# First modulation of a spectral adaLN block folded into the Fourier table, grad_out transposes regrouped, x held on chip

## The chip, the cores and the metric

The kernel runs on one core of a Trainium2 chip. A core has five engines with a queue each: TensorE (PE, with its weight loads PEld), VectorE (DVE), ScalarE (ACT), GpSimd (POOL) and SyncE (SP), which issues most of the transfers. The metric is the device time of one execution in microseconds (us).

## The reference

The program returns the output of one block and its gradients for eight inputs, given `grad_out`. The block, cut to what matters:

```
mod = silu(c) @ w_mod                 # 6 vectors of 576: sa, ca, ga, sb, cb, gb
h = layernorm(x) * (1 + ca) + sa
x = x + ga * irfft2(rfft2(h) * (w_r + 1j*w_i))
h = layernorm(x) * (1 + cb) + sb
x = x + gb * (((h @ w_gate) * (h @ w_up)) @ w_down)
```

`x` and `grad_out` are 2048 x 576 in bfloat16, `w_gate` and `w_up` 576 x 4608, `w_down` 4608 x 576, `w_mod` 576 x 3456. The outputs are the block's result and the gradients of x, w_r, w_i, w_gate, w_up, w_down, c and w_mod.

## The kernel before, in words

The 2048 rows are dealt to 128 partitions and 16 tiles t, so that a tile is 128 rows by 576 columns. The Fourier transform over rows and columns is done as matrix products with tables.

**The head** (lines 288 to 461) is the part the change touches. The vector c is loaded (lines 291, 292), passed through the sigmoid, and spread over 128 columns per block of 128 values (`sc_rep`, line 308). `mod_load` (310) loads one sixth of w_mod as five blocks of 128 rows, `mod_make` (316) multiplies it, which gives a modulation vector repeated on all 128 partitions (`modh`), in two halves of 288 columns and five blocks each, thus ten products; it is also stored to memory (325) for later stages.

Then stage 1 runs as a software pipeline of three steps over the 16 tiles. `s1_norm` (359) takes the statistics of x (`norm_stats`, 175: six numbers per half row, a merge, a square root on ScalarE, a reciprocal and a product), normalises on ScalarE (372), multiplies by 1 + ca and adds sa on VectorE (374, 376), stores the normalised x (378), turns the tile with five transposes on PE (381) and copies it out on ScalarE (`hT`, 383). `s1_cols` (385) multiplies by the column table `RD`: ten products of 292 columns, five for the real and five for the imaginary part (390); ScalarE copies both to `zt` (391). `s1_rows` (400) multiplies by the row table `G1`, four products (404, 405), and ScalarE and VectorE copy one half each into `VA` (406). With tile 1, the gate vector gb is made too (394), stored, and read back as a column (`gbT`, 396 to 398).

**grad_out** is loaded in three pieces (349), turned tile by tile, six transposes each (421), and scaled by gb on VectorE into `goT` (422). A row has 576 = 4 x 128 + 64 columns; the fifth transpose gives the last 64 on partitions 0 to 63, and a sixth, of columns 448 to 575, gives them again on partitions 64 to 127, which line 423 scales. Later products for the upper blocks of w_down (from `TWICE` = 20 on) use the two copies side by side (444 to 447). In the earlier blocks the rows of w_down's transpose that meet the second copy are zero, from zeros that line 285 writes beside the loaded rows of `wdn`.

**After stage 1**, stage 2 turns each of 19 chunks of `VA` (477), transforms it (485), multiplies by the filter (492 to 497), turns it back (503) and transforms it back (511). Between the chunks groups of products goT x w_down (`u4_group`, 428; the product is line 451) fill PE; their result `ghh_st` goes to memory. Stage 3 (536 to 580) returns to rows (210 to 216), copies to `ut` (541, 542) and `yb` (552), and `s3_norm` (554) forms the second residual: it loads x again into `xc` (560), computes yb x ga + x (565, 566), takes statistics, normalises (570), and modulates into `h2p` (572 to 574). The long gated part follows, from line 583 to the end of its loop, and then the gradients' way back.

What sets the order: a scheduler places the instructions of each engine at build time from their data dependences and priorities. The function `in_order` (159) pins a list of one engine's instructions in the order given, and `issue_after` queues the instructions that its block traces on the same engine behind a given one; neither makes an engine wait at run time. `mod_make`'s store of the second vector is that instruction (`first`, 344) for most of SP's later loads. Transfers of the SP queue are issued in order, and one that must wait holds back those behind it.

## Time and profile before

| | |
|---|---|
| median of 3 runs | 1526.43 us (1525.81 to 1529.65) |
| profiled execution | 1524.87 us |
| its span, first to last instruction | 1523.1 us |
| mean granted TensorE clock | 0.996 |
| PE busy | 1490.3 us, 98% of the span |
| VectorE busy | 1060.6 us, 70% |
| ScalarE busy | 583.4 us, 38% |
| first column product of line 390 | 16.02 us |
| last, of tile 15 | 61.16 us |

How to read it: all times in a profile count from the first instruction of the profiled execution. A share of busy time is an average over the whole span; stages with different limits are read from the windows of the trace, which give each engine's busy time in a stretch. A line of the timeline gives start, duration, engine, source line, operation, output and inputs, and in square brackets how long the engine was idle before it and what ended the wait. A duration includes the time in which the next instruction has started already, so where a queue is full the distance from start to start is what an instruction costs.

### The profile page before, as it was taken

To read this page: it belongs to the slowest core of one execution; us is meant where nothing else is said; L and a number is where in the kernel's file an instruction comes from. 1 tells how busy PE (TensorE), PEld (TensorE's weight loads), DVE (VectorE), ACT (ScalarE), POOL (GpSimd) and SP (SyncE) were. 2 spreads that over 40 slices of the span, in tenths; PEclk is the share of its full clock that TensorE was granted. 3 is DMA by queue.
4 is the path that set the end of the run, shared out by engine and by line. 5 is a ranking of instruction groups with operands and counts; after the bars stand their busy time and mean duration, and the time that the engine had idled before them with its cause. 6 is when DMAs were issued, how large, how long until landed. Compare 5 with 4: busy or idle time off the path is not lost. (4 is left out here: it accounts for less than half of the span.)

```text
span 1523.1 us, 29031 instructions
## 1 busy us (share of the span) xinstructions
PE 1490.3 (98%) x11140; PEld 1012.6 (66%) x11144; DVE 1060.6 (70%) x2646; ACT 583.4 (38%) x1189; POOL 238.8 (16%) x363
## 2 busy tenths in 40 slices
PE   6899999999999999999999999999999999999998
PEld 4666543566666667666666676676666667888876
DVE  6866753666677767667677677676676768688884
ACT  6667742322222222222222222222222225686763
POOL 0001222101101102111111120120110113221022
PEclk9999999999999999999999999999999999999999
DMA  8968999688878768768778588688677779965587
GB/s 317 282 200 224 278 255 249 152 162 155 174 129 161 155 125 174 152 125 177 135 146 178 118 159 164 119 163 156 137 152 153 132 175 252 305 220 181 182 290 201
DMA packets 487181, 280.42 MB, mean 184 GB/s; under 512 B 408865, under 2 KB 457378, under 8 KB 486018
## 3 DMA queue, kind: packets, MB, share of 16 engines
q1 hardware_dynamic: 458882, 175.32, 55.6%
q0 software_dynamic: 28160, 103.25, 23.0%
q8 instruction: 87, 1.43, 0.4%
q14 instruction: 52, 0.43, 0.1%
HBM read 108.62 MB, written 82.31 MB: 125 GB/s over the span
## 5 line engine op out<-in xcount | busy, mean ns | idle before, releaser
L752 DVE TENSOR_TENSOR acc<-acc,u8p 128x288 f32<-128x288 f32 (+1 forms) x1088 | 483.3, 453 | 276.1 <-PE u8p L747 272.6
L747 PE MATMUL u8p<-wT,ggT 128*128 128x288 bf16 x1152 | 328.0, 286 | 1.7 <-DVE acc L752 1.6
L747 PE MATMUL u8p<-wT,guT 128*128 128x288 bf16 x1152 | 327.6, 286 | 0.0
L711 PE MATMUL gup<-h2T,wgu 128*128 128x512 bf16 x1152 | 297.8, 379 | 0.0
L646 ACT CAST so<-u57p 128x288 bf16<-128x288 f32 x216 | 86.3, 400 | 532.8 <-PE u57p L644 522.1
L644 PE MATMUL u57p<-h2p,gu_sf 128*128 128x288 bf16 x1152 | 186.4, 286 | 0.0
L644 PE MATMUL u57p<-h2p,gg_sf 128*128 128x288 bf16 x1152 | 185.9, 286 | 0.0
L711 PEld LDWEIGHTS <-wgu 128*128 128x128 bf16 x1152 | 109.6, 98 | 97.9 <-issue 17.1
L747 PEld LDWEIGHTS <-ggT 128*128 128x128 bf16 x1152 | 112.6, 98 | 66.5 <-issue 14.0
L451 PE MATMUL u4p<-goT,wdT 128*128 128x512 bf16 x656 | 151.1, 379 | 0.9 <-DVE goT L423 0.5
L747 PEld LDWEIGHTS <-guT 128*128 128x128 bf16 x1152 | 112.7, 98 | 57.6 <-issue 2.4
L1286 PE MATMUL u3p<-wd,hl 128*128 128x288 bf16 x936 | 141.3, 288 | 0.1
L713 ACT CAST gT<-gup 128x512 bf16<-128x512 f32 x144 | 84.5, 587 | 131.5 <-PE gup L711 129.6
L644 PEld LDWEIGHTS <-hh_sf 128*128 128x128 bf16 x1152 | 112.7, 98 | 28.4
L644 PEld LDWEIGHTS <-gu_sf 128*128 128x128 bf16 x1152 | 112.4, 98 | 28.5
L644 PEld LDWEIGHTS <-gg_sf 128*128 128x128 bf16 x1152 | 112.4, 98 | 28.2
L1286 PEld LDWEIGHTS <-hl 128*128 128x128 bf16 x1152 | 107.8, 98 | 25.7 <-DMA hl<-hhT_d 0.4
L713 ACT CAST uT<-gup 128x512 bf16<-128x512 f32 x144 | 84.5, 587 | 77.4 <-PE gup L711 77.4
L451 PEld LDWEIGHTS <-wdT 128*128 128x128 bf16 x656 | 61.3, 98 | 73.0 <-issue 7.6
L644 PE MATMUL u57p<-gonC,hh_sf 128*128 128x288 bf16 x576 | 99.7, 286 | 0.0
L724 POOL DMA_DIRECT2D hhT_d<-hhT x36 | 33.3, 925 | 375.5 <-DVE hhT L715 352.5
L173 DVE CAST ghh_st<-u4p 128x512 bf16<-128x512 f32 x56 | 38.7, 691 | 59.0 <-PE u4p L451 58.9
(373 smaller groups left out, 1867.6 us busy)
## 6 DMA issues: line engine op xcount, KB each, us to landing
ghhT_d<-ghh_st POOLq DMA_DIRECT2D x36, 512.0 KB, 4.3
ghh<-ghhT_d POOLq DMA_DIRECT2D x36, 512.0 KB, 7.3
hhT_d<-hhT POOLq DMA_DIRECT2D x36, 512.0 KB, 6.4
hl<-hhT_d SPq DMA_DIRECT2D x28, 576.0 KB, 6.0
out_dram<-woT SPq DMA_DIRECT2D x70, 128.0 KB, 2.0
wdn<-in_B_w_down_dram SPq DMA_DIRECT2D x18, 288.0 KB, 3.6
wd<-in_B_w_down_dram POOLq DMA_DIRECT2D x36, 144.0 KB, 4.7
out_dram<-so SPq DMA_DIRECT2D x36, 144.0 KB, 2.8
```

Of the source, the lines that this page charges most:

```text
L173: nc.vector.tensor_copy(dst, src)
L451: nc.tensor.matmul(pt[:], lhsT=wdTs[k][:, j, m, :], rhs=goT[:, 4 * sb4:4 * sb4 + 4, m, :], start=(m == 0 and n == 5), stop=(m == n - 1))
L644: mm = nc.tensor.matmul(pw[0][:, 0:288], lhsT=sf[:, t, :], rhs=rhs_n(t, h * 288, 288), start=(t == 0), stop=(t == NT - 1))
L646: followed(mm, nc.scalar.copy(so[:, h * 288:(h + 1) * 288], pw[0][:, 0:288]))
L711: nc.tensor.matmul(pts[k][:], lhsT=wgu[:, 4 * wi_ + m, jw * 128:(jw + 1) * 128], rhs=h2T[:, ts_, m, :], start=False, stop=(m == 3))
L713: nc.scalar.copy((gT, uT)[wi_][:, th_, :], pts[k][:])
L724: nc.gpsimd.dma_start(hhT_d[:, :, fb, :].rearrange("tp f x -> f tp x"), hhT[:].rearrange("f (tp ti) p -> f tp (ti p)", ti=2))
L747: nc.tensor.matmul(pu[:, 0:288], lhsT=l_, rhs=r_, start=(k == 0), stop=(k == len(mms) - 1))
L752: summed[t] = nc.vector.tensor_tensor(out=ghb(t)[:, hs_] if fbs[-1] == NFB - 1 else dst, in0=dst, in1=pu[:, 0:288], op=ADD).ins
L1286: mm = nc.tensor.matmul(p2[ti][:, 0:288], lhsT=hls[fb // 9][:, fb % 9, ti * 128:(ti + 1) * 128], rhs=w[:, fb - f0, h * 288:(h + 1) * 288], ...
```

## The change

- **The scale goes into the table, the shift into a row.** The normalised tile is no longer multiplied by 1 + ca and shifted by sa. Instead the column table is scaled, row by row, by 1 + ca (`RDs`), which is possible because the table's rows are the tile's columns. To have 1 + ca and sa along partitions, new products with one moving column each are made (`mod_cols`, 25 per vector). The tile buffers `n1r` have ones in columns 576 and 608, which become rows 64 and 96 of the fifth block, and the table gets there the product of sa with `RD`, in two bfloat16 parts. The repeated vector 1 + ca is still made and stored; the repeated sa is not.
- **grad_out is turned five times instead of six.** Tiles whose number divided by four is odd take columns 448 to 575 in the fifth transpose, the others columns 512 to 639, and `gbT` holds a scale column for each case, with zeros where the other half lies, so one scaling per tile remains. `gbT` now comes from one-column products and no longer from memory. The last 64 rows of w_down's blocks are therefore loaded twice in all blocks, not only from the twentieth on.
- **x stays on chip.** All of x is loaded into `h2p`, which stage 3 reads in place of `xc`.
- Beside these: 56 products of the unit matrix with itself at the start, whose result is not used; `G1` loaded in two parts; the copies of line 406 moved to VectorE for half of the tiles; the order of PE in the prologue and of some of VectorE's instructions pinned; the sigmoid ahead of the first square root.

```diff
+        n1r = [hw2.tile([128, 4, DP], BF, name="n1r%d" % k, bufs=1) for k in range(2)]
+        for n_ in n1r:
+            nc.gpsimd.memset(n_[:, :, D:DP], 0.0)
+            nc.gpsimd.memset(n_[:, :, D:DP:32], 1.0)
...
+        warm = fps.tile([128, 512], FP32, name="warm", tag="fp")
+        with tc.high_priority(60):
+            for _ in range(56):
+                nc.tensor.matmul(warm[:, 0:128], lhsT=ident[:], rhs=ident[:], start=True, stop=True)
...
+        def mod_cols(wm):
+            ps = fps.tile([128, 512], FP32, name="modc", tag="fp")
+            for d in range(5):
+                w = min(128, D - 128 * d)
+                for m in range(5):
+                    nc.tensor.matmul(ps[0:w, d:d + 1], lhsT=wm[:, m, 128 * d:128 * d + w], rhs=sc_bf[:, m:m + 1], start=(m == 0), stop=(m == 4))
+            return ps, ((slice(0, 128), slice(0, 4)), (slice(0, 64), slice(4, 5)))
+
+        def x_load(t0, t1):
+            nc.sync.dma_start(h2p[:, t0:t1, 0:D], x_v[:, t0:t1, :])
...
+        def scaled_table():
+            ps, parts = mod_cols(wms[MCA])
+            for r, k in parts:
+                one = nc.vector.tensor_scalar(out=opca_c[r, k], in0=ps[r, k], scalar1=1.0, scalar2=None, op0=ADD)
+            for m in range(5):
+                r = slice(0, min(128, D - 128 * m))
+                nc.vector.tensor_scalar(out=RDs[r, m].rearrange("p c f -> p (c f)"), in0=T["RD"][r, m].rearrange("p c f -> p (c f)"), scalar1=opca_c[r, m:m + 1], scalar2=None, op0=MUL)
+            return one.ins
+
+        def shift_rows():
+            ps, parts = mod_cols(wms[MSA])
+            for r, k in parts:
+                nc.vector.tensor_copy(msl[r, k, 64:128:32], ps[r, k].unsqueeze(2).to_broadcast([r.stop, k.stop - k.start, 2]))
...
+            for cc in range(2):
+                zp = fps.tile([128, 512], FP32, name="zms", tag="fp")
+                for m in range(5):
+                    nc.tensor.matmul(zp[:, :FP], lhsT=msl[:, m, :], rhs=T["RD"][:, m, cc, :], start=(m == 0), stop=(m == 4))
+                nc.scalar.copy(RDs[64:65, 4, cc, :], zp[64:65, :FP])
+                nc.vector.tensor_copy(hi[96:97, cc, :], zp[96:97, :FP])
+                nc.vector.tensor_tensor(out=RDs[96:97, 4, cc, :], in0=zp[96:97, :FP], in1=hi[96:97, cc, :], op=SUB)
...
-            nm = hw2.tile([128, D], BF, name="nm")
-            nc.vector.tensor_tensor(out=nm[:], in0=n1[:, tt, :], in1=modh[MCA][:], op=MUL)
-            hh = hpp[:, t % 3, :]
-            nc.vector.tensor_tensor(out=hh[:, 0:D], in0=nm[:], in1=modh[MSA][:], op=ADD)
...
-                    mm = nc.tensor.matmul(zp[:, :FP], lhsT=hTs[t][:, m, :], rhs=T["RD"][:, m, cc, :], start=(m == 0), stop=(m == 4))
+                    mm = nc.tensor.matmul(zp[:, :FP], lhsT=hTs[t][:, m, :], rhs=RDs[:, m, cc, :], start=(m == 0), stop=(m == 4))
...
-                evac(Vv[:, :, t, cc, :], vp[:, :FP].rearrange("k (g f) -> k g f", f=4), eng=("a" if cc == 0 else "v"))
+                evac(Vv[:, :, t, cc, :], vp[:, :FP].rearrange("k (g f) -> k g f", f=4), eng=("a" if cc == 0 and t % 2 else "v"))
+
+        s1_norm(0)
+        mod_make(MCA, wms[MCA])
+        mark1 = traced()
+        shift_rows()
+        dve0 += on_dve(mark1)[0:2]
+        s1_cols(0)
+        in_order(pe_since(mark))
+        mark = traced()
+        pipeline(NT, [lambda t: s1_norm(t) if t else None, lambda t: s1_cols(t) if t else None, s1_rows])
+        in_order(dve0 + on_dve(mark)[0:9])
...
-            pt = u4ps.tile([128, 6, 128], BF, name="u4p")
-            for m in range(6):
-                nc.tensor.transpose(pt[:, m, :], gon(t, m * 128 if m < 5 else 448, 128), ident[:])
-            nc.vector.tensor_tensor(out=goT[:, t, :, :], in0=pt[:, 0:5, :], in1=gbT[:].unsqueeze(2).to_broadcast([128, 5, 128]), op=MUL)
-            nc.vector.tensor_tensor(out=goT[64:128, t, 4, :], in0=pt[64:128, 5, :], in1=gbT[64:128, 4:5].to_broadcast([64, 128]), op=MUL)
+            odd = t // 4 % 2
+            pt = u4ps.tile([128, 5, 128], BF, name="u4p")
+            for m in range(5):
+                nc.tensor.transpose(pt[:, m, :], gon(t, m * 128 if m < 4 or not odd else D - 128, 128), ident[:])
+            nc.vector.tensor_tensor(out=goT[:, t, :, :], in0=pt[:], in1=gbT[:, odd, :].unsqueeze(2).to_broadcast([128, 5, 128]), op=MUL)
...
-                    if fb >= TWICE:
-                        nc.sync.dma_start(wdn[:, :, D:DP], rows[:, :, 512:D])
+                    nc.sync.dma_start(wdn[:, :, D:DP], rows[:, :, 512:D])
...
-            xc = hw2.tile([128, 2, D], BF, name="xc")
-            nc.sync.dma_start(xc[:], x_v[:, s0:s0 + 2, :])
...
-                nc.vector.tensor_tensor(out=x1[:, i, :], in0=x1[:, i, :], in1=xc[:, i, :], op=ADD)
+                nc.vector.tensor_tensor(out=x1[:, i, :], in0=x1[:, i, :], in1=h2p[:, s0 + i, 0:D], op=ADD)
```

More of the change, by code (lines that the diff above doesn't have):

```diff
@@ L295, in build @@
         sig = hp1.tile([128, 5], FP32, name="sig")
-        nc.scalar.activation(out=sig[:], in_=c_f[:], func=ACT.Sigmoid)
-        nc.vector.tensor_tensor(out=sc_col[:], in0=c_f[:], in1=sig[:], op=MUL)
+        gated = nc.scalar.activation(out=sig[:], in_=c_f[:], func=ACT.Sigmoid).ins
+        sc_bf = hp1.tile([128, 5], BF, name="sc_bf")
+        nc.vector.tensor_tensor(out=sc_bf[:], in0=c_f[:], in1=sig[:], op=MUL)
         tmp5 = hp1.tile([128, 5], FP32, name="tmp5")
@@ L302, in build @@
         nc.vector.tensor_tensor(out=dsl_col[:], in0=tmp5[:], in1=sig[:], op=MUL)
-        sc_bf = hp1.tile([128, 5], BF, name="sc_bf")
-        nc.vector.tensor_copy(sc_bf[:], sc_col[:])
         nc.vector.tensor_copy(sc_col[:], sc_bf[:])
@@ new lines, in build, with s1_stats, on_dve @@
+        n1s = {}
+        def s1_stats(t):
+            n = 1 if t == 0 else 4 - t % 4
+            nmr = norm_stats(h2p[:, t:t + n, 0:D], hw2, n, "ln1", rstd1g[:, t:t + n], 4)
+            for k in range(n):
+                n1s["nmr", t + k] = nmr[:, k:k + 1]
+        def on_dve(mark):
+            return [i for i in nc.cur_bb.bb.instructions[mark:] if i.engine == mybir.EngineType.DVE]
+        mark = traced()
+        s1_stats(0)
+        nmr0 = on_dve(mark)[-1]
+        in_order([gated, rooted[0]])
@@ L394, in s1_cols @@
                     mod_make(MGB, wms[MGB], "a")
-                with nc.allow_non_contiguous_dma(reason="tiny column load"):
-                    nc.sync.dma_start(gbT[:, 0:4], modb_d[0, MGB, 0:512].rearrange("(m q) -> q m", q=128))
-                    for r in (0, 64):
-                        nc.sync.dma_start(gbT[r:r + 64, 4:5], modb_d[0, MGB, 512:576].rearrange("(m q) -> q m", q=64))
+                ps, parts = mod_cols(wms[MGB])
+                for r, k in parts:
+                    for odd in range(2):
+                        if k.start < 4 or not odd:
+                            nc.vector.tensor_copy(gbT[r, odd, k], ps[r, k])
+                ps = fps.tile([128, 512], FP32, name="modc", tag="fp")
+                for m in range(5):
+                    nc.tensor.matmul(ps[:, 0:1], lhsT=wms[MGB][:, m, D - 128:D], rhs=sc_bf[:, m:m + 1], start=(m == 0), stop=(m == 4))
+                nc.vector.tensor_copy(gbT[64:128, 1, 4:5], ps[64:128, 0:1])
         def s1_rows(t):
```

80 lines of the change are left out of this document (41 added, 39 removed).

## The prediction

> **What bounds the kernel now.** I cut the span into stages first, at the start of the first column product (16.00), of the third (24.95), of the last (61.16), and at the first turn of a filtered chunk (76.04, line 503). The columns are the stretch, its length, and the busy us of PE, PEld, DVE, ACT and POOL, then the granted clock, the DMA share and GB/s.
>
> ```profile
> 0.00:16.00 16.00, 5.15 (x25) 2.96 (x25) 9.10 (x42) 8.33 (x13) 1.57 (x12) 0.97 0.85 298
> 16.00:24.95 8.95, 8.49 (x53) 5.75 (x54) 5.71 (x19) 5.08 (x12) 0.71 (x1) 0.68 1.03 385
> 24.95:61.16 36.21, 32.99 (x300) 24.23 (x301) 31.68 (x84) 30.98 (x67) 3.37 (x5) 1.00 0.94 292
> 61.16:76.04 14.88, 12.54 (x105) 7.53 (x103) 11.90 (x26) 5.96 (x12) 0.53 (x1) 1.00 0.80 271
> 76.04:160.00 83.96, 83.96 (x655) 51.83 (x654) 54.94 (x158) 58.26 (x118) 10.76 (x20) 1.00 0.76 218
> 160.00:200.00 40.00, 37.59 (x248) 23.11 (x247) 29.44 (x96) 30.39 (x63) 10.29 (x19) 1.00 1.08 276
> ```
>
> PE is full from 76.04 to 160 and nearly full afterwards, so whatever time PE saves before 76.04 lasts to the end. The order of PE's matmuls in the built kernels is the same in both from that turn on. There are two places to gain: the head, and the idle 2.4 us of 160 to 200. For the second, PE's waits there, and the wait for the tile `xc`:
>
> ```profile
> PE yp L216 <- ACT ut L171: 1.8, 2, 1.3
> PE yp L216 <- DVE ut L173: 0.6, 1, 0.6
> ```
> ```profile
>   DMA xc<-in_A_x_dram: 5.0, 4
> ```
>
> VectorE waits four times, 5.0 us together, for x read a second time (line 560); `ut` and the norms queued behind line 566 come late, and PE with them.
>
> Inside the middle stage one tile costs 2.53 us at best, and that is a loop between ScalarE and PE, not PE's work. In the timeline:
>
> ```profile
> 30.98 1.42 PE L390 MATMUL zp<-T_RD,hT 128*128 128x292 bf16 x10
> ...
> 32.43 0.40 ACT L171 CAST zt<-zp 128x292 bf16<-128x292 f32 x1 [0.22 <-PE zp L390]
> ...
> 32.77 0.69 ACT L171 COPY hT<-trp 128x640 bf16<-128x640 bf16 x1
> ...
> 33.51 1.42 PE L390 MATMUL zp<-T_RD,hT 128*128 128x292 bf16 x10
> ```
>
> Products at 30.98, second `zt` 1.45 later, `hT` 0.34 after it, next products 0.74 after that: 2.53. A normalisation (line 372, 0.77 from start to start) ahead of the first `zt` fits into ScalarE's idle time; one between the two `zt` lengthens the loop.
>
> **The head, walked anew.** Durations are rows of this execution; the order of each engine is that of the built kernel.
>
> *A, to the second tile's norm.* The removed steps are the 20 products of line 320 for the first two vectors (10 stay), the shift of line 376 and the scale of line 374 (32 VectorE operations, 14.6 us). Their place is taken by 56 warm-up products while PE idles for loads (the first products of before started at 6.85; 56 at the cold pitch of 0.11 end near 7.5), then 25 one-column products for each vector, five table scalings, ten products of the shift row with the table and six small row operations. A one-column product I take at 0.06, the warm start-to-start of line 381's 128-column transposes, between nothing less than that weight load and the cold 0.11. Column products of the first vector run 7.4 to 8.9; transposes, 10 products (1.22) and the second vector's columns end at 12.1. A scaling of 584 elements has no row: from 0.22 (line 308) to 0.82 (line 422); I take 0.25, as both operands lie in SBUF as in line 308. The table lands near 11.0 (12.06 in before, now with 432 KB less ahead), scalings end at 12.2, the ten products at 13.9. VectorE then has a statistic of tile 4 queued ahead of the row operations, and that waits for x of tiles 4 to 7: 3,706 KB into a queue that moved 1,536 KB from 12.06 to 15.74, thus 14.4. From there copy (0.46), statistic (0.39), subtraction (0.46), twice, end at 17.25, so the first column product is complete at 17.4, against 18.6. But the statistics of tiles 1 to 3 now follow: seven operations to 19.1, square root 0.30, reciprocal, statistic, product to 20.2; normalisation 0.87; transposes of tile 1 start at **21.0**. In before they started at 18.4.
>
> *B, 21.0 to the third column product.* PE has no gap: 5 transposes 0.30, four row products 0.49, 8 transposes of grad_out 0.49 (the load is due at 20.7: 6,154 KB, where before had 6,442 KB at 21.9), column product 1.22, ten products of the gate vector 1.22, 30 one-column products 1.80, transposes 0.30, row products 0.49, 7 transposes 0.43: 6.74 at full clock. The clock is the doubt:
>
> ```profile
> 8.08:11.49 3.41, 2.90 (x13) 1.67 (x12) 3.09 (x11) 0.17 (x1) 0.00 (x0) 1.00 1.10 434
> 11.49:14.90 3.41, 1.02 (x10) 0.48 (x7) 1.46 (x7) 3.23 (x6) 0.00 (x0) 1.00 0.96 402
> 14.90:18.32 3.42, 2.30 (x10) 1.46 (x11) 2.43 (x6) 2.24 (x4) 0.71 (x1) 0.50 1.03 349
> 18.32:21.73 3.41, 3.41 (x19) 2.12 (x18) 1.55 (x5) 1.73 (x4) 0.00 (x0) 0.50 1.05 359
> ```
>
> A stretch of 3.41 us with PE busy 1.02 was followed by half clock; 2.30 did not end it, 3.41 did, and 2.90 had released it earlier. In A, PE works about 1.2 us between 14.0 and 21.0, so half clock is due when B starts, and it lasts until a stretch that PE fills, beginning somewhere in the 3.4 us after about 20.2, has passed: 1.4 to 3.1 lost, mean 2.2. The third product starts at 21.0 + 6.7 + 2.2 = **29.9** (before: 24.95). The Trainium skill, "TensorE: Matmul & The Clock Gate", section "What's actually happening", says that the clock is halved after at least one idle window of about 3.4 us in a free-running grid. Read as a wholly idle window it would hardly ever strike here and B would lose nothing; the trace's window with 1.02 busy speaks against that reading.
>
> *C, third to last column product.* By ScalarE's order: five loops with two normalisations or one between the `zt`s (3.0, 2.92, 3.0, 3.0, 2.70), the other eight at 2.53: 34.9. VectorE's 16 statistics (0.39) and its other rows from 29.3 put the fourth grad_out product at 41.6, and PE's ten transposes queued there wait about 1.0 (nothing to 2.0). So 35.9 (before 36.2), and the last product starts at 65.8. The loop of ScalarE stays; that is where the 14.6 us of VectorE go: beside it.
>
> *D, last product to the turn at 76.04.* Before, 33 of 96 grad_out transposes were still to come and PE waited for lines 422 and 423; the 30 products of line 451 followed them. After, all 80 are done, line 423 (16 at 0.29) is gone and two of the 30 products too: last row products 2.27 in, 15 products 3.34, 4 transposes 0.25, 4 products 0.89, 0.50, 6 products 1.34, 0.50: 9.1, against 14.9. The turn comes at **74.9**: the head gains **1.1**.
>
> *Queues.* SP now issues x of tiles 4 to 7 and the rest of the row table ahead of the second half of the prologue, since they stand behind an instruction of VectorE and no longer behind the stores of line 325. The gate vector's load waits for its buffer until PE's ten products at 10.4, the grad_out loads behind it; with 4,858 KB issued by then the transfers do not run dry. The gate vector's store (needs ScalarE, near 28) holds x of tiles 12 to 15 to a landing near 33; VectorE wants it near 36. The three column loads of `gbT` and SP's 6.1 us wait for them go; its values now come from the 30 one-column products in B. POOL's six added memsets are short (0.14 to 0.30 in its rows) and over before 4. The eight evacuations of line 406 moved from ScalarE to VectorE (0.46 each) are in C's sums.
>
> **x kept.** The eight loads of `xc` go and with them the 5.0 us of VectorE's waits; PE's 2.41 idle go if no other wait is next. From 184 on, with `xc` early, a tile takes 3.93 without a gap, ScalarE's and VectorE's work fitting in. I take **2.4** (bounds 0 and 2.4). The ten added loads of 64 columns (0.47 of the SP queue, 3.5 to landing in line 438's rows) precede transposes whose result is ready near 53 and wanted near 60: nothing, unless they were 7 us later.
>
> **Sum.** 1.1 + 2.4 = 3.5. The profiled execution took 1524.87 (span 1523.1), so 1521.4 of that kind; the median of the runs shown, 1526.43, is 1.56 higher: **1522.9**. About 0.3%, 4.6 us, is what a measurement can tell from no change.
>
> **Rivals.**
> 1. *The clock stays full.* For it: the warm-up products, and column products filling PE until 12.1. Against: the window of 1.02. B loses nothing, the head gains 3.3, but VectorE's wait in C takes 0 to 1 more; in all 5.7: 1520.7.
> 2. *Slower: one-column products do not count as work for the clock.* They use one column of the moving operand, and no row shows one. Place: half clock from about 11, so the second vector and the row products take 1.85 longer ahead of 17.25, and B stays cold throughout, 6.7 lost instead of 2.2. That is 6.4 worse, 1529.3; it decides once more than 3.5 us beyond my 2.2 are lost. Against: 128-column weight loads run all along, and the longer products between them are counted.
> 3. *x kept does nothing:* the norms then wait for the next thing, the ScalarE order around line 570. Head alone: 1525.3. Against: all three PE waits follow a wait for `xc`.
>
> **Chances.** Forecast 0.50 (0.14 of it over 4.6 faster, 0.01 slower), rival 1 0.25 (0.22 faster), rival 2 0.15 (half of it slower by 4.6, 0.07), rival 3 0.10 (0.01 slower). Faster 0.36, same 0.55, slower 0.09. For the range: forecast ±2 from the clock's phase, the wait in C and the scalings (0.25 to 0.82 costs up to 1.9 behind the landing at 14.4), extended to rival 1 with a short wait below and over rival 3 above: 1519.3 to 1527.0; the far part of rival 2 stays out.
>
> **What would show it.** The first column product complete near 17.4 and tile 1's transposes near 21; half clock over the third product's approach; third product 29.9, last 65.8, first turn 74.9; no wait for `xc` and no idle PE between 160 and 200. A third product before 28, or one after 32, or PE waits of another name in the norms would prove the sum wrong.

## The result and the profile after

The changed kernel takes 1521.61 us (median of 8 executions, 1519.33 to 1524.64), the kernel before beside it 1530.11 (8 executions, 1524.49 to 1535.08): ratio 0.9946 (95% interval 0.9925 to 0.9968). It is **faster, by 0.54%**, a small gain; a ratio of 1 lies outside the interval. The time foretold, 1522.9, is 1.3 above the median and the range holds it; but the gain in medians is 8.5 us where the sum said 3.5. The two profiled executions differ by only 1.4 us (1523.45, span 1521.7, against 1524.87, span 1523.1). So the sum was right neither about the medians nor about that pair, and the question is why in both.

First the stages of the changed kernel. They are cut at 16.00 as before, and then where the prediction's steps end: tile 1's transposes start at 22.60 (end of A), the third column product at 30.11 (B), the last at 65.11 (C), the first turn at 74.10 (D). The columns are those of the first table of the prediction: stretch, length, busy us of PE, PEld, DVE, ACT, POOL, granted clock, DMA share, GB/s.

```profile
0.00:16.00 16.00, 11.96 (x135) 9.80 (x135) 6.16 (x35) 6.34 (x10) 2.96 (x17) 0.89 0.86 306
16.00:22.60 6.60, 1.22 (x6) 0.51 (x7) 6.41 (x22) 2.02 (x5) 0.00 (x0) 0.73 1.05 415
22.60:30.10 7.50, 7.50 (x83) 6.10 (x83) 3.19 (x13) 6.01 (x12) 0.91 (x1) 0.78 0.73 257
30.10:65.10 35.00, 33.84 (x316) 25.29 (x315) 25.99 (x64) 27.44 (x58) 2.82 (x4) 1.00 0.97 284
65.10:74.10 9.00, 8.96 (x63) 5.05 (x62) 3.69 (x10) 4.66 (x10) 1.77 (x2) 1.00 0.74 253
74.10:158.10 84.00, 84.00 (x654) 51.83 (x655) 56.87 (x165) 58.95 (x120) 11.90 (x22) 1.00 0.83 230
158.10:198.10 40.00, 40.00 (x262) 24.63 (x261) 32.10 (x102) 32.03 (x65) 10.83 (x20) 1.00 1.08 272
```

The last row answers to 160 to 200 of before: PE busy 40.00 of 40.00 instead of 37.59, and in PE's waits none is left for `yp`. The first turn is 1.94 earlier (74.10 against 76.04). The last product of stage 3 comes 4.9 earlier (start of the last `yp` product 194.73 against 199.60), and the gated products (lines 770 and 775) start 5.2 earlier, 267.60 against 272.78. That lead is still whole 990 us later, at the first column sum with `n2c` (line 979): 1256.78 against 1261.98. But the span is only 1.4 shorter. The rest of the lead is lost **after** 1256, in two places (3.1 and 1.6; after them 0.9 comes back, as the part behind 1486 takes 35.5 instead of 36.4). The first is in PE's waits (engine, line and operation, what it waited for; us, times, longest), at the top of the list:

```profile
PE csC L979 <- DMA yc<-y_d: 2.9, 1, 2.9
PE trp L434 <- ACT n1r L429: 2.8, 1, 2.8
PE spp L991 <- ACT dmb L1003: 2.7, 1, 2.7
PE zp L443 <- DVE RDs L387: 2.7, 2, 2.1
PE zms L384 <- DVE msl L379: 2.3, 1, 2.3
```

The first line has no counterpart in before: PE waits 2.9 for one load of `yc`, and the column sums take 69.92 from first to last instead of 66.86. The second place is the clock. The third line, a wait that before has too (2.4), leaves PE idle near 1470. In stretches on the clock's own grid, after and then the changed kernel with whole rows (an experiment below):

```profile
1469.70:1473.10 3.40, 1.36 (x10) 0.78 (x7) 3.26 (x9) 0.00 (x0) 1.37 (x2) 1.00 1.06 404
1473.10:1476.50 3.40, 2.72 (x9) 1.71 (x10) 3.26 (x10) 3.14 (x6) 0.00 (x0) 0.50 0.75 238
1476.50:1479.90 3.40, 3.40 (x16) 2.11 (x14) 2.51 (x7) 3.32 (x7) 0.57 (x1) 0.50 0.73 229
```
```profile
1465.90:1469.30 3.40, 1.81 (x13) 1.14 (x11) 3.26 (x9) 0.00 (x0) 1.56 (x2) 1.00 1.08 406
1469.30:1472.70 3.40, 2.53 (x18) 1.96 (x19) 3.26 (x9) 2.95 (x6) 0.00 (x0) 1.00 0.78 257
1472.70:1476.10 3.40, 3.40 (x30) 2.71 (x28) 2.54 (x8) 3.32 (x7) 0.37 (x1) 1.00 0.74 243
```

About the same idle time lies inside one stretch in the first (1.36 busy, then half clock for two stretches) and across two in the second (1.81 and 2.53 busy, clock full). From the last of those column sums to the first `spp` product of `dsa` (line 991) it takes 156.2 in the second kernel, 157.9 in before (one stretch at half clock) and 159.5 in after (two). All fourteen profiles lie between 156.2 and 159.7. In twelve of them that wait is 2.3 to 2.7, and the time goes by the number of stretches at half clock alone: 156.2 or 156.3 with none (four profiles), 157.7 to 158.1 with one (seven), 159.5 with two (after). The two kernels without the warm-up products wait 3.5 and 3.8 and take 159.4 and 159.7 with one. So the second place is where the grid stands against the idle time in that execution, and not something that the change did. The Trainium skill, "TensorE: Matmul & The Clock Gate", section "What's actually happening", says that the window is about 3.4 us long and free-running; these rows agree. It gives an idle window as the cause of half clock; here 1.36 busy us in the window did not prevent it.

### The profile page after: what moved, and what is told of

It reads as the page before. It is cut to its first block, busy times and chain, and to the rows that moved or that the text cites. A ratio compares the mean times of both kernels' runs of the same rounds, so it can differ in the third digit from the quotient of the medians.

```text
span 1521.7 us, 29239 instructions
## 1 busy us (share of the span) xinstructions
PE 1495.4 (98%) x11260; PEld 1020.0 (67%) x11264; DVE 1048.5 (69%) x2620; ACT 580.3 (38%) x1182; POOL 241.0 (16%) x368
```

## The experiments

**The theories after this result.** X: `xc` costs more than the 2.4 of one profile, because the time of its loads differs from execution to execution. The rival is that the head gives the rest. In the first two recorded expectations X is called rival A; their own theory T, that the profiled pair tells the whole gain and that its late loss is chance, is the first thing to be tested. For the late loss, P: the five memsets that the change added on POOL shift its queue. R: the change makes POOL's queue hand out more rows, which moves a pause of that queue. Medians below are of as many executions as are given; before ran beside each group (medians 1525.88 to 1528.98, single executions 1521.37 to 1537.74).

### x kept alone, and x not kept

**Only x kept** (before, with this one part of the change):

```diff
-            xt = hw2.tile([128, 4, D], BF, name="xt", bufs=3)
+            xt = h2p[:, 4 * c4:4 * c4 + 4, 0:D]
...
-            nc.sync.dma_start(xc[:], x_v[:, s0:s0 + 2, :])
...
+                nc.vector.tensor_tensor(out=x1[:, i, :], in0=x1[:, i, :], in1=h2p[:, s0 + i, 0:D], op=ADD)
```

> The kernel before with one part of the change: all of x is loaded into h2p and stage 3 reads it there; xc and its eight loads are gone. Theory T (the lead of the profiled pair at the start of the gated part, 5.2 us, is the lasting gain: 1.9 from the head and about 3.0 from stage 3; what the pair lost again after 1257 us, 2.9 in a wait for yc and 1.7 in one more stretch of half clock, is chance of one execution): first turn of a filtered chunk at 76.0 as before, no PE wait for ut, last product of stage 3 (yp) at 196.6 in place of 199.6, and 3.0 us less than before in the medians. Rival A (the eight loads cost much more in most executions than in the profiled one, which is why the medians differ by 8.5): 6 to 8 us less than before, and a narrower spread of its times. Rival B (x kept does nothing, the norms wait for the next thing): within 1 us of before, yp at 199.

Measured: 1519.28 (1518.49 to 1519.96, 12), ratio 0.9952 (0.9933 to 0.9971); before beside it 1526.52. That is 7.2 us, three times the term of the sum. The spread fell from 16 us (before, 35 executions) to 1.5. Theory T had the events right (last `yp` product at 196.5, foretold 196.6, no wait for `ut`), but its 3.0 for the medians is refuted.

**x reloaded** (after, with that part undone):

```diff
+            xc = hw2.tile([128, 2, D], BF, name="xc")
+            nc.sync.dma_start(xc[:], x_v[:, s0:s0 + 2, :])
...
-                nc.vector.tensor_tensor(out=x1[:, i, :], in0=x1[:, i, :], in1=h2p[:, s0 + i, 0:D], op=ADD)
+                nc.vector.tensor_tensor(out=x1[:, i, :], in0=x1[:, i, :], in1=xc[:, i, :], op=ADD)
```

> The changed kernel, but stage 3 loads x again into xc as before. Theory T: first turn at 74.1 as in the changed kernel, VectorE waits for xc some 5 us and PE for ut some 2 to 3 us, last yp at 197.7; 1.9 us less than before in the medians, about 3 more than the changed kernel. Rival A (the loads of xc are what mattered): 0 to 2 us less than before, 6 to 8 more than the changed kernel. Rival B: the same as the changed kernel, 5 to 8 less than before.

Measured: 1526.00 (1522.98 to 1530.29, 12), ratio 0.9990 (0.9971 to 1.0010): without x kept nothing measurable is left of the change. (This kernel has the head's gain and the late loss too, so it says nothing of either alone.) VectorE's timeline of this kernel (start, us, line, operation, in brackets the idle time before it and what ended it), and PE's waits:

```profile
142.78 0.46 DVE L632 TENSOR_TENSOR x<-x,xc 128x576 bf16<-128x576 bf16 x1 [4.81 <-DMA xc<-in_A_x_dram]
...
183.01 0.46 DVE L632 TENSOR_TENSOR x<-x,xc 128x576 bf16<-128x576 bf16 x1 [1.49 <-DMA xc<-in_A_x_dram]
...
194.82 0.46 DVE L632 TENSOR_TENSOR x<-x,xc 128x576 bf16<-128x576 bf16 x1 [4.16 <-DMA xc<-in_A_x_dram]
```
```profile
PE yp L218 <- ACT ut L171: 3.3, 3, 1.3
PE yp L218 <- DVE ut L173: 3.3, 2, 2.3
```

The same eight loads in the same stage: VectorE waits 12.9 us in four places where the profile of before had 5.0 in four, PE 6.6 where before had 2.4, and a load lands after 6.5 (median; longest 10.3) instead of 4.9 (6.4). The DMA share of that stage is 1.1, so a reload takes what the other transfers leave it. From the first to the last `yp` product the stage takes 63.0 in before, 67.5 here, and 60.0 or 60.1 in every kernel with x kept. X holds: one part of the change, in the old head, gives 7.2 of the 8.5, so the rival falls. That the time of the loads differs so much is read from two profiles and from the spread of the run times; which other transfers hold them up stays open.

### The head

**grad_out turned six times again** (after, with the fifth and sixth transpose, the second scaling, and w_down's second load only from the twentieth block on):

```diff
+        nc.gpsimd.memset(wdn2[:, :, :, D:DP], 0.0)
...
-            pt = u4ps.tile([128, 5, 128], BF, name="u4p")
-            for m in range(5):
-                nc.tensor.transpose(pt[:, m, :], gon(t, m * 128 if m < 4 or not odd else D - 128, 128), ident[:])
+            pt = u4ps.tile([128, 6, 128], BF, name="u4p")
+            for m in range(6):
+                nc.tensor.transpose(pt[:, m, :], gon(t, m * 128 if m < 4 else (512 if m == 4 else D - 128), 128), ident[:])
...
+            nc.vector.tensor_tensor(out=goT[64:128, t, 4, :], in0=pt[64:128, 5, :], in1=gbT[64:128, 1, 4:5].to_broadcast([64, 128]), op=MUL)
...
-                    nc.sync.dma_start(wdn[:, :, D:DP], rows[:, :, 512:D])
+                    if fb >= TWICE:
+                        nc.sync.dma_start(wdn[:, :, D:DP], rows[:, :, 512:D])
```

> The changed kernel, but grad_out is turned six times a tile and scaled in two instructions, as before, and the last 64 rows of w_down's blocks are loaded twice only from the twentieth on. PE has 16 transposes more (0.06 each, 1.0 us) and two products moved back behind the last column product (0.45), VectorE 16 scalings more (0.29 each, 4.6). Theory T1 (after the last column product PE is the bound): last column product within 0.5 of 65.1, first turn 1.0 to 2.0 later than 74.1, total 1 to 2 us more than the changed kernel. Rival (VectorE is the bound again there, PE waits for goT as in the kernel before): first turn at 76 or later, 2 to 4 us more. Rival (it lies in gaps of PE between the column products): nothing, 74.1.

Measured: 1522.99 (1520.26 to 1536.64, 12), ratio 0.9984 (0.9959 to 1.0008). The median is 1.4 above that of after, less than the spread; the profile is the better witness. The first turn comes 2.7 later than in after (76.77, foretold 75.1 to 76.1), and with PE idle for only 0.4 behind the last column product: PE's own work sets that stretch, and theory T1 had its size too small. Stage 3's first product starts at 137.32, against 134.66 in after: turning five times instead of six is worth 2.7 in the head. And 137.32 is 0.9 later than with only x kept (136.40). So the first modulation in the table and the row, with all that it needs in the prologue, **costs** about 0.9, and the head's whole gain comes from the turns. Each of these starts is one profile's; kernels with the same head differ by up to 0.8 (134.36 to 135.1 in three with the changed head, 135.8 to 136.6 in four with the old one), so the cost of the modulation is 0.7 to 1.5.

**The order of VectorE in the prologue** (after; shift rows ahead of tile 4's statistic, and grad_out's first transposes behind the products of tile 1):

```diff
...
-        dve0 += on_dve(mark1)[0:2]
+        rows = on_dve(mark1)
...
-        in_order(dve0 + on_dve(mark)[0:9])
+        in_order(dve0[0:3] + rows[0:2] + dve0[3:] + rows[2:] + on_dve(mark)[0:11] + n1s["first", 4])
...
+            if t == 0:
+                in_order([n1s["cols", 1], pe_since(turned)[0]])
```

> The changed kernel with another order of VectorE in the prologue: the shift's columns (msl) ahead of the table scalings, the row operations behind them, and no statistic of tiles 4 to 7 ahead of the norm of tiles 1 to 3; the first transposes of grad_out stand behind the second tile's column products. Theory T (the chain of VectorE up to the second tile's norm sets the head's end, and each us of it lasts): ten products of the shift row at 10.8 (12.44 in the changed kernel), first column product complete at 15.6 (19.8), transposes of tile 1 at 18.6 (22.6), third column product at 26.5 (30.1), first turn at 70.5 (74.1), 3.5 us less than the changed kernel. Rival 1 (the loads bound it: grad_out landed at 21.9, the gate vector's part of w_mod near 20.5): third column product at 28.5, first turn at 72.5, 1.5 less. Rival 2 (PE's clock falls to half in the emptier prologue and stays there through B): third column product at 29 or later, nothing gained.

Measured: 1520.71 (1517.53 to 1525.45, 12), ratio 0.9950 (0.9928 to 0.9973). Timelines of PE (first two lines) and VectorE:

```profile
18.64 0.71 PE L436 MATMUL trp<-ident,n1r 128*128 128x128 bf16 x5 [4.28 <-ACT n1r L431]
...
27.64 1.41 PE L445 MATMUL zp<-RDs,hT 128*128 128x292 bf16 x10
```
```profile
28.91 0.46 DVE L183 BATCH_NORM_STATS2 ln_st<-h2p 128x6 f32<-128x288 bf16 x1 [2.08 <-DMA h2p<-in_A_x_dram]
```

Tile 1's transposes start 4.0 earlier than in after and the third column product 2.5 earlier, but then VectorE waits 2.08 for x of tiles 8 to 11, the last column product starts at 65.19 (65.11 in after), the first turn comes at 75.04 where theory T had 70.5, and stage 3 begins at 135.59, 0.9 later than in after. The gain is lost between 28 and 65 us. That this one load takes it was the next guess; the experiment with the loads moved, below, does not bear it out.

**No warm-up products** (after without the 56):

```diff
-        warm = fps.tile([128, 512], FP32, name="warm", tag="fp")
-        with tc.high_priority(60):
-            for _ in range(56):
-                nc.tensor.matmul(warm[:, 0:128], lhsT=ident[:], rhs=ident[:], start=True, stop=True)
```

> The changed kernel without the 56 products of the unit matrix; the order of grad_out's transposes among PE's other work shifts with it (the first eight behind the second tile's column products). With them, the profile shows the clock at full from 5.4 to 12.2. Theory W (they only bring the full clock forward over 50 one-column products and ten products that wait for loads and VectorE anyway): the ten products of the shift row at 12.4 as before, first column product complete within 0.5 of 19.8, the third column product within 1 us of 30.1, median within 1 us of the changed kernel's 1521.6. Rival (without them the prologue and B run at half clock for longer): the shift row's products 1 us later, third column product at 32 or later, 2 us more.

Measured: 1520.54 (1518.42 to 1521.57, 12), ratio 0.9944 (0.9923 to 0.9965), no slower than after. The one-column products take 1.32 and 1.07 instead of 1.16 and 0.89, but another order of VectorE comes out of the scheduler, which does not wait there for x (in after it waits 1.03 and 1.60 us); tile 1's transposes start at 20.23 and the gated products at 266.41, 1.2 earlier than in after. This experiment changes two things at once, so it says only that the 56 products buy nothing here.

### The late loss

POOL's timeline of only-x-kept, then of after: a store of `hhT_d`, and two transfers of the loop whose `yc` came late:

```profile
1233.15 0.91 POOL L722 DMA_DIRECT2D hhT_d<-hhT  x1 [1.03 <-DVE hhT L713]
...
1268.21 0.55 POOL L987 DMA_DIRECT2D gx_d<-gxr  x1 [2.68 <-DVE gxr L879]
1269.80 0.98 POOL L1062 DMA_DIRECT2D wd<-in_B_w_down_dram  x1 [1.05 <-PE vp L1023]
```
```profile
1232.21 0.91 POOL L788 DMA_DIRECT2D hhT_d<-hhT  x1 [1.83 <-DVE acc L816]
...
1266.46 0.55 POOL L1053 DMA_DIRECT2D gx_d<-gxr  x1 [2.67 <-DVE gxr L945]
1267.18 0.98 POOL L1128 DMA_DIRECT2D wd<-in_B_w_down_dram  x1 [0.17 <-DMA out_dram<-so]
```

The load of 1,008 KB of w_down follows the store ahead of it after a pause of 1.05 in the first and 0.17 in the second. Counted from the first of the column sums, it starts 11.3 after it in the first (and in before), 10.4 in after, while the store of `hhT_d` some 35 us earlier shows the opposite: 25.4 ahead of the column sums in the first, 24.6 in after. So a pause of 0.9 has moved from one transfer to another. The releaser in the bracket of the first is no explanation: in after the same load starts at 1267.18, ahead of the `vp` product (1267.57) that the first seems to wait for.

**The five memsets on VectorE** (after; theory P), and **five memsets added on POOL** (to only-x-kept, on a tile that nothing reads):

```diff
-            nc.gpsimd.memset(n_[:, :, D:DP], 0.0)
-            nc.gpsimd.memset(n_[:, :, D:DP:32], 1.0)
+            nc.vector.memset(n_[:, :, D:DP], 0.0)
+            nc.vector.memset(n_[:, :, D:DP:32], 1.0)
...
-        nc.gpsimd.memset(msl[:], 0.0)
+        nc.vector.memset(msl[:], 0.0)
```
```diff
+        idle = hw2.tile([128, 5, 64], BF, name="idle", bufs=1)
+        for k in range(5):
+            nc.gpsimd.memset(idle[:, k, :], 0.0)
```

> The changed kernel with five of its short memsets (n1r four, msl) on VectorE in place of POOL, so that POOL has as many instructions ahead of the late part as in the kernel before (368 in place of 373). What it asks: all four profiles with the changed head show a slow stretch of transfers 10 to 30 us after the first product of the column sums (csA), yc landing in up to 10.5 us, w_down's load issued 10.4 us after csA; both with the old head show that load at 11.3 and yc in 6.8, though the orders of all engines are the same there. Theory P (the place of POOL's instructions in its stream decides when that load goes out, and the two loads then meet or miss woT's transfers): the load at 11.3, yc in at most 8.6, no PE wait for yc, hl or wd in the column sums, times within 2 us of one another and a median 2 to 3 us under the changed kernel's, near 1518.5. Rival (SP's longer list of transfers, or chance of the stretch before): the load at 10.4, PE waits of 0.4 to 3 us as before, median near 1521.5 and a spread of 5 us or more.

> The kernel before with x kept in h2p (as in e1_x_kept) and five memsets of an unused tile on POOL at the start, nothing else: POOL has 373 instructions instead of 368. Theory P: w_down's load goes out 10.4 us after csA in place of 11.3, yc takes up to 10 us, the spread of the times grows from 1.5 us to 4 or more and the median from 1519.3 by 1 to 3 us. Rival: nothing changes, 11.3 and 1519.3 with a spread under 2 us.

Measured: without them on POOL 1519.97 (1517.99 to 1523.77, 12), ratio 0.9956 (0.9939 to 0.9973), the load still at 10.4; with them added 1519.42 (1518.07 to 1520.37, 12), ratio 0.9945 (0.9927 to 0.9964), the load still at 11.3. Theory P falls, from both sides: the place of the load did not move. The first kernel's profile shows no PE wait for `yc`, `hl` or `wd`, and its median is 1.6 under that of after, so the size of the late loss differs between kernels with the same head and the load at the same place.

**The rows of a store, in the kernel without the change's head** (only-x-kept with the tile `n1` 640 wide, so that the four stores to `n1_d` are 512 rows of 1,152 bytes each instead of 128 of 4,608; each engine's order is that of only-x-kept):

```diff
-                n1s[c4] = hw2.tile([128, 4, D], BF, name="n1")
+                n1s[c4] = hw2.tile([128, 4, DP], BF, name="n1")
...
-            nc.scalar.activation(out=n1[:, tt, :], in_=xts[c4][:, tt, :], func=ACT.Identity, bias=n1s["nmr", t], scale=rstd1g[:, t:t + 1])
+            nc.scalar.activation(out=n1[:, tt, 0:D], in_=xts[c4][:, tt, :], func=ACT.Identity, bias=n1s["nmr", t], scale=rstd1g[:, t:t + 1])
...
-                nc.gpsimd.dma_start(n1_d[:, t - 3:t + 1, :], n1[:])
+                nc.gpsimd.dma_start(n1_d[:, t - 3:t + 1, :], n1[:, :, 0:D])
```

> The kernel of e1_x_kept with one thing of the changed head: the normalised x lies in a buffer 640 columns wide, so that each of POOL's four stores to memory consists of 4 x 128 rows of 1,152 bytes instead of 128 rows of 4,608. Orders and waits of all engines are those of e1_x_kept. Theory R (the number of rows that POOL's queue has handed out, 1,536 more from here on, decides at which of its later transfers it pauses for 0.9 us; with the old count that is the load of w_down 11.3 us after csA, with the new one the store of hhT 25 us ahead of it): the load goes out at 10.4, the store at -24.6, yc takes up to 10 us, the spread of the times grows from 1.5 us to 4 or more and the median from 1519.3 by 1 to 3. Rival (another part of the changed head: SP's list, the wider weights, the time at which the late part comes): 11.3, -25.4, yc at most 7, 1519.3 and a spread under 2.

Measured: 1522.26 (1519.72 to 1525.66, 12), ratio 0.9960 (0.9941 to 0.9979). The median is 3.0 above only-x-kept and the spread 6 instead of 1.5; ten of the twelve executions are longer than the longest of only-x-kept. The load is now at 10.4, the store at 24.6 ahead, as theory R foretold. POOL's rows of this kernel, to be read beside those of only-x-kept above, and the line that PE's waits gain:

```profile
1233.37 0.91 POOL L722 DMA_DIRECT2D hhT_d<-hhT  x1 [1.83 <-DVE acc L750]
...
1268.35 0.98 POOL L1062 DMA_DIRECT2D wd<-in_B_w_down_dram  x1 [0.17 <-DMA out_dram<-so]
```
```profile
PE csC L913 <- DMA yc<-y_d: 0.7, 1, 0.7
```

These are not the only two places. Four more stores of `hhT_d`, between 319 and 1043 us, show the same shift in the idle time ahead of them: near 320 us 18.03 in only-x-kept and 19.82 here, near 348 us 1.88 and 0. At these six transfers all fourteen profiles fall into the same two groups.

**Whole rows in the changed kernel** (after, with `n1_d` 640 wide in memory, so that a store is 128 rows of 5,120 bytes):

```diff
-    n1_d = dram("n1_d", [128, NT, D], BF)
+    n1_d = dram("n1_d", [128, NT, DP], BF)
...
-                nc.gpsimd.dma_start(n1_d[:, t - 3:t + 1, :], n1[:, :, 0:D])
+                nc.gpsimd.dma_start(n1_d[:, t - 3:t + 1, :], n1[:])
...
+                nc.sync.dma_start(ld3[k][:], src[:, sa, 0:D])
```

> The changed kernel with the store of the normalised x as whole rows of 640 columns into a buffer in memory that is as wide, so that each of the four stores is 128 rows again (of 5,120 bytes); it is read back in rows of 576 columns. Theory R: the load of w_down at 11.3 after csA, yc at most 7 us, no PE wait for yc, hl or wd in the column sums, spread under 2.5, median 1517.5 (1519.3 less the 1.75 us by which the changed head leads until there). Rival: 10.4 and 1521 with a spread of 5, as in the changed kernel.

Measured: 1517.07 (1516.43 to 1519.65, 7), ratio 0.9932 (0.9905 to 0.9959), 4.5 below after, of whose eight executions seven are longer than the longest here; the load at 11.3, the store at 25.4 ahead, no wait for `yc`. Only the spread, 3.2, is wider than the 2.5 that R allowed. The transfers issued from 1262 to 1274 (KB each, median us to landing), in after and then here:

```profile
wd<-in_B_w_down_dram POOLq DMA_DIRECT2D x1, 1008.0 KB, 12.4
...
n2c<-n_d SPq DMA_DIRECT2D x2, 144.0 KB, 6.5
...
woT<-so SPq DMA_TRANSPOSE x1, 10.2
```
```profile
wd<-in_B_w_down_dram POOLq DMA_DIRECT2D x1, 1008.0 KB, 7.6
...
n2c<-n_d SPq DMA_DIRECT2D x2, 144.0 KB, 5.1
...
woT<-so SPq DMA_TRANSPOSE x1, 5.4
```

At 10.4 the load starts 0.2 ahead of the transposing load `woT` (10.6 in after), and both take about twice their time; at 11.3 `woT` goes first. The `yc` and `n2c` loads among them come late with them. This holds in every profile: in the seven with the load at 10.4 it takes 11.1 to 12.7 us and `woT` 10.2 to 12.3; in the six at 11.3 it takes 6.8 to 7.8 and `woT` 3.6 to 6.5; in the kernel without warm-up products, where the load starts at 10.8 and 0.15 behind `woT`, they take 8.7 and 8.4. Of the eight that are not at 11.3, six show a wait of 0.4 to 2.9 for `yc` or `wd` in their profile, and a seventh 0.4 for `hl`; of the six at 11.3 none does. R holds in both directions: an edit of the four stores (1,536 rows more, or whole rows again) brings the loss into one kernel and takes it out of the other. That it is the count of the rows, and not their length of 1,152 bytes, is argued and not shown, for the two edits change both; why the queue pauses where it does stays open.

### Put together

**Loads ahead of grad_out** (the order of VectorE, memsets on VectorE, and x of tiles 8 to 15 issued after the first piece of grad_out), the same **with whole rows**, and the kernel with whole rows alone **without the warm-up products**. The lines that move the loads:

```diff
-            x_load(8, 12)
+                if t0 == 0:
+                    x_load(8, 12)
+                    x_load(12, NT)
...
-            if t == 4:
-                with tc.issue_after(first):
-                    x_load(12, NT)
```

> The kernel of e5_rows_first (row operations first, grad_out's first transposes behind the second tile's column products) with x of tiles 8 to 15 loaded ahead of the second and third piece of grad_out, and the five memsets on VectorE. In e5_rows_first the transposes of tile 1 came at 18.6, as expected, but VectorE waited at 28.9 for x of tiles 8 to 11 and the last column product came no earlier (66.3). Theory L (that load is what took the gain back): no wait for x at 28.9, last column product near 62.5, first turn near 71, stage 3's last product near 192; 2 to 3 us less than the changed kernel, and with theory P near 1516. Rival 1 (ScalarE's loop and the clock, which stood at half from 35.4 for 3.4 us in e5_rows_first, take it back anyway): last column product at 65 or later, nothing gained in the head. Rival 2 (the later pieces of grad_out are now late: PE waits for gonB near 30): last product near 64.5.

> The kernel of e8_loads_order with the store as in e10_n_padded. Theory R: the load at 11.3, no late PE wait for yc, wd or hl, spread under 2.5; the head as in e8_loads_order, whose gated part started at 267.2 against 269.4 in e1_x_kept, so 2.1 us under 1519.3: a median near 1517. Rival: 1519 with a spread of 6, as e8_loads_order.

> The kernel of e10_n_padded without the 56 products of the unit matrix, as in e3_no_warm: the two edits that helped most, together, and the price of those products without the late waits. In e3_no_warm the third column product started at 28.6 against 30.1, and the gated part at 266.4 against 267.6. Theory: the load of w_down at 11.3 after csA, the gated part at 266.4, no late PE wait for a transfer, spread under 3, and a median about 0.9 us under e10_n_padded's 1517.1, near 1516.2. Rival (the lead of 1.2 us in the head does not last, or hangs on the pause's place): 1517 or more, or a spread of 4 or more.

Measured: 1518.99 (1517.88 to 1523.98, 12), ratio 0.9952 (0.9934 to 0.9971); 1517.16 (1516.39 to 1517.84, 8), ratio 0.9924 (0.9898 to 0.9949); 1518.53 (1517.32 to 1519.52, 6), ratio 0.9944 (0.9923 to 0.9966). With the loads moved, theory L fails: the last column product starts at 64.51 (foretold 62.5) and the first turn comes at 73.72 (foretold 71), with VectorE now waiting 3.22 for a load of x at 23.27. (The 66.3 that the expectation gives for the last column product of the kernel it starts from is 65.19 in the trace.) Stage 3 begins at 134.28, 0.4 earlier than in after, and the gated products start at 267.37 with whole rows, where whole rows alone have 267.31: nothing came of the order. The warm-ups again: without them the gated products start only 0.2 earlier (267.15), and the median is 1.5 higher instead of the 0.9 lower that was foretold, with a longer wait (for `dmb`, 3.8 instead of 2.5) and a stretch at half clock near 1473 that the kernel with them does not have. Whole rows take 1.8 off the median of the kernel with the loads moved (1518.99 to 1517.16) and 2.0 off that of the one without warm-up products (1520.54 to 1518.53), less than the 4.5 in after. The best here are the changed kernel with whole rows (1517.07) and the same with the loads moved (1517.16); the two cannot be told apart.

## Why the prediction was right, and where it was wrong

**The time was right by two errors that cancel.** In medians: x kept 7.2 instead of 2.4; the head 2.2 (from 1519.28 to the 1517.07 with whole rows) instead of 1.1; a late loss of 4.5 (1517.07 to 1521.61) that no step of the sum and no rival had. The first is 4.8 more than forecast and the last takes 4.5 back; that they nearly cancel is luck. Together 4.9, to which 3.6 come that lie in before itself: its median was 1526.43 in the runs shown, 1526.52 beside the first experiments, and 1530.11 with the five further executions beside the result.

**x kept: the step that failed** is "I take 2.4 (bounds 0 and 2.4)". The upper bound was the idle time of PE in one execution. The mechanism was right: no `xc`, no wait for `ut`, PE full. But a wait for a transfer in a stage with a DMA share of 1.08 is a sample, and it was taken from one of before's quick executions (1524.87, of 1521.37 to 1537.74). Even there the stage gained 2.9 (63.0 to 60.1): 2.4 of idle time, all of it inside the forty microseconds that were counted, and 0.5 of busy time, as the same 400 products count 60.59 busy us in before, with three stops among them, and 60.07 in after.

**"Whatever time PE saves before 76.04 lasts to the end"** failed second. The order of PE is indeed the same, and the 5.2 lasted for 990 us. But the argument looked at PE's order only. POOL's queue had the same transfers in the same order, with other rows. The added columns of `n1r` made the store of `n1_d` a store of pieces; the full change shows that in one slice (`n1[:, :, 0:D]` in the store), and the prediction did not count it. The last 1.6 were the clock's grid, which lay differently in every profile.

**A, second tile's norm: 1.6 late** (transposes at 22.60, foretold 21.0). PE's and VectorE's timelines of after:

```profile
9.30 0.89 PE L347 MATMUL modc<-sc_bf,wm 128*128 128x1 bf16 x25
12.44 2.61 PE L384 MATMUL zms<-T_RD,msl 128*128 128x292 bf16 x10 [2.25 <-DVE msl L379]
```
```profile
10.79 1.49 DVE L373 TENSOR_SCALAR RDs<-T_RD,opca_c 128x584 bf16<-128x584 bf16 x5 [2.69 <-DMA T_RD<-tab_RD]
...
15.88 0.46 DVE L183 BATCH_NORM_STATS2 ln_st<-h2p 128x6 f32<-128x288 bf16 x1 [1.60 <-DMA h2p<-in_A_x_dram]
...
18.84 0.47 DVE L387 TENSOR_TENSOR RDs<-zms,hi 1x292 bf16<-1x292 f32 x1
```

The unknown durations were sized well: one-column products 0.89 for 25, 0.036 each (I took 0.06), a scaling of 584 elements 0.30 from start to start (0.25), five done at 12.28 (12.2). The wait for tile 4 was foreseen in kind, but the wait ends at 15.88, not 14.4, and these 1.5 are nearly the whole of the 1.6: the row operations behind it took 0.6 longer than forecast, and the statistics and the product after them 0.6 less. The first column product is complete at 19.8 (foretold 17.4). The ten products of the shift row took 2.61 instead of 1.22, since the clock was halved already at 12.2, sooner than forecast; they ended at 15.05, ahead of that x, and cost nothing.

**B, 1.4 short** (7.5, forecast 8.9), so the third product came at 30.11 where 29.9 stood. The clock on its grid, in after:

```profile
5.39:8.80 3.41, 3.28 (x58) 2.85 (x57) 0.99 (x8) 2.14 (x4) 0.00 (x0) 1.00 1.10 407
8.80:12.21 3.41, 1.39 (x31) 1.17 (x28) 1.42 (x6) 1.09 (x3) 0.00 (x0) 1.00 1.02 392
12.21:15.62 3.41, 3.18 (x14) 1.95 (x14) 1.04 (x5) 0.79 (x2) 0.00 (x0) 0.50 1.07 424
15.62:19.03 3.41, 1.07 (x7) 0.40 (x5) 3.00 (x8) 0.40 (x1) 0.00 (x0) 1.00 1.04 398
19.03:22.44 3.41, 0.42 (x1) 0.11 (x1) 3.38 (x15) 1.46 (x3) 0.00 (x0) 0.50 1.05 434
22.44:25.85 3.41, 3.25 (x21) 2.58 (x22) 2.18 (x9) 2.62 (x5) 0.73 (x1) 0.50 0.99 367
```

Each stretch with 0.4 to 1.4 busy is followed by half clock, those with 3.2 by full. (The clock column prints 1.00 until the first change on record. In before, the first ten products of line 320, from 6.85, took 2.56, where ten at full clock take 1.2 to 1.4: so the clock stood at half there, and the stretch with 2.90 busy in the prediction did release it.) B began at half clock as forecast, but 22.60 happened to lie just behind the start of a window, so it lost 1.6 and not the mean of 2.2; the one-column products at 0.036 instead of 0.06 saved most of the rest. The late A and the short B are one thing in part, and that they cancel is luck.

**C and D held.** C took 35.0 (35.9): the wait of 1.0 for VectorE's scalings did not come, inside the 0 to 2.0 given. The loops of ScalarE set the pace as worked out. D took 9.0 (9.1). The head's 1.9 are nearer the forecast 1.1 than rival 1's 3.3. The prediction did not ask which edit gives them: the turns give 2.7, the modulation takes 0.9.

**The rivals.** 1, clock full: refuted by the rows above. 2, one-column products not counted as work: no more than 1.6 was lost in B, so its slow outcome did not come. Whether they count stays open: the window 5.39 to 8.80 holds 1.1 us of them, but without them 2.2 busy would be left, and 1.81 sufficed in the rows near 1466. 3, x kept does nothing: refuted by the first experiment. None of them reached past 200 us, and that is where the unforeseen term was.

## What to carry to other kernels

A wait for a transfer in a stage whose DMA engines are full is worth more than one profile shows, and its bound should come from the spread of the run times as much as from the trace: 16 us of spread that shrank to 1.5 was the sign of it. Where a change pads a tile that a store reads, count the store's rows before and after, and keep them whole: here that alone decided 1.8 to 4.5 us, 1,200 us later. Before a change is kept as one piece, take each part out once: the parts here were a gain of 7.2 (x kept), one of 2.7 (the turns), about nothing (the warm-up products), and two losses (the modulation about 0.9, the store of pieces 1.8 to 4.5).

## What was not expected of the hardware

- POOL's DMA queue pauses about 0.9 us at places that move with the rows of its earlier transfers: four stores with 1,536 rows more, some 1,200 us earlier, moved a pause from one transfer to another. In medians that is 3.0 us where the rows were added, and 4.5, 2.0 and 1.8 in the three kernels where they were made whole.
- A load of 1,008 KB that starts 0.2 us ahead of a transposing load took 12.4 instead of 7.6 us, and the transposing one 10.2 instead of 5.4.
- The same idle time of PE halved the clock or not by where it lay on a grid of 3.41 us: 1.36 busy in one stretch did, 1.81 and 2.53 in two did not. With that, 156.2 to 159.5 us passed for the same work.
- 25 one-column products with their weight loads run at 0.036 us each at full clock.
